# One output projection, two matmul shapes: sixteen 512-column products and a VectorE add in place of sixty-four 128-column products

## The chip, the core and the metric

The kernel runs on one core of a Trainium2 chip. The metric is device time in microseconds (us). A run with a profile also gives a trace; its span (about 656.5 us here) is a little shorter than the device time of the same run (about 658.3 us), since it goes from the first instruction to the last. PE is TensorE, PEld its weight loads, DVE is VectorE, ACT is ScalarE, SPq the queue from which SyncE issues DMA.

## The reference

One decode step: layer norm of a row of 512, then the sum of the row itself, a cached attention block and a dense block.

```python
# x: 1 x 512; wq: 512 x 4096; wo: 4096 x 512
# k_cache, v_cache: 8 groups x 65536 keys x 128; 32 heads, 4 heads in each group
xn = layernorm(x)
q = xn @ wq
o = softmax(q @ K.T / sqrt(128)) @ V          # for each of the 32 heads
out = x + o.reshape(1, 4096) @ wo + gelu(xn @ w1 + b1) @ w2 + b2
```

K and V are 268 MB in bfloat16, wo is 4.2 MB. The step studied here is `o @ wo`, a row of 4096 times a 4096 x 512 matrix, at the very end.

## The kernel before

K and V stream through four SBUF slots while PE transposes K, makes scores and accumulates P times V. The dense branch is finished at the start. Its 512 outputs (with x and b2 in them) wait in `f_rows` as four partial rows, on partitions 0, 32, 64 and 96, with zeros between.

wo is the last thing loaded. It arrives in five pieces: three for the first seven groups (16, 8 and 4 heads: `wo0`, `wo1`, `wo2`) and two for the last group (three heads and one: `wl0`, `wl1`).

```python
def dma_wo():                                       # ... shortened
    for i, (g0, n) in enumerate(WP):                # WP: 4, 2 and 1 groups
        sch.dma(SP, ..., wsem[i], writes=[f"wo{i}"] + (["slot0"] if i == 0 else []))
    for i, n in enumerate(WH):                      # WH: 3 heads and 1
        sch.dma(SP, ..., lsem[i], writes=[f"wl{i}"] + (["slot1"] if i == 0 else []))
```

The tail then multiplies. The stationary operand is one column (one head's share of o), the moving operand a strip of wo. Each of the four 128-column strips of the output goes to its own PSUM partition (0, 32, 64 or 96), called a column group here. Products of the four groups run together in the trace of this kernel: the first four start between 649.637 and 649.657 us, and one takes about 0.31 us. Everything accumulates in one PSUM row per strip, and one VectorE copy and one DMA end the kernel.

```python
def fin_mm(kt, lhsT, rhs, reads, first, last, publish):
    sch.op(PE, lambda: pe.matmul(pR[32 * kt:32 * kt + 1, 0:128], lhsT=lhsT, rhs=rhs, start=first, stop=last), ...)

for kt in range(KT):                                # KT = 4: add the dense branch
    fin_mm(kt, ones_f[:, 0:1], f_rows[:, kt * 128:(kt + 1) * 128], ["f_rows", "ones_f"], True, False, kt == KT - 1)
for i, (g0, n) in enumerate(WP):                    # 64 + 32 + 16 products
    for r in range(g0 * HPG, (g0 + n) * HPG):
        for kt in range(KT):
            fin_mm(kt, oX_bf[:, r:r + 1], wo_sb[:, r, kt * 128:(kt + 1) * 128], ["oX", f"wo{i}"], False, False, ...)
for h in range(HPG):                                # last group: 16 products
    for kt in range(KT):
        fin_mm(kt, oT_all[:, ...], wl_sb[:, h, kt * 128:(kt + 1) * 128], ["oL", "wl0 or wl1"], False, h == HPG - 1, ...)
sch.op(DVE, lambda: dve.tensor_copy(out=fin_bf[0:NR, :], in_=pR[0:NR, 0:128]), ...)   # then the output DMA
```

## Time and profile before

| | before |
|---|---|
| time, median of 3 runs | 658.36 us (658.20 to 658.52) |
| span of the trace | 656.5 us |
| busy: PE, VectorE, ScalarE | 82%, 42%, 37% |
| main DMA queue, share of 16 engines | 99.2% |

PE looks busy, but the DMA engines are the ones that never rest. This is one line of the page's table of DMA queues (queue, packets, MB, share of the 16 engines' span), and the line that sums up HBM traffic:

```profile
q1 hardware_dynamic: 8616, 280.50, 99.2%
...
HBM read 280.50 MB, written 0.00 MB: 427 GB/s over the span
```

The chain of waits (start in us, length, what) ends like this. It is followed backwards from the last instruction, so the first line is what the end was waiting for:

```profile
636.99 16.42 DMA kv<-in_A_wo_dram
653.41 0.14 issue
653.55 0.63 PE pss L805 x13
...
654.20 0.29 DVE fin_bf L820
```

653.41 is the landing of `wl0`. The last piece, `wl1`, lands at 653.73 by the same trace (issued at 637.42, 16.31 us to landing). After these two only the last products, one copy and the output DMA are left. The timeline of the same stretch shows what PE did until then (start, length, engine, line, operation, operands, count, and in brackets the idle time just before with what ended it). A product in fp32 shows as two passes, so the four products with `f_rows` are eight:

```profile
649.26 0.61 PE L805 MATMUL pss<-f_rows,ones_f 128*1 128x128 f32 x8
...
649.64 3.41 PE L805 MATMUL pss<-kv,oX_bf 128*1 128x128 bf16 x112
...
652.45 0.31 PEld L805 LDWEIGHTS pss<-kv,oX_bf 128*1 128x1 bf16 x16 [0.32 <-DMA kv<-in_A_wo_dram]
...
653.55 0.59 PE L805 MATMUL pss<-kv,oT_all 128*1 128x128 bf16 x16 [0.50 <-DMA kv<-in_A_wo_dram]
654.20 0.29 DVE L820 CAST fin_bf<-pss 97x128 bf16<-97x128 f32 x1 [4.13 <-PE pss L805]
```

PE waited twice for wo: 0.32 us for the third piece (seen at the weight loads) and 0.50 us for the last pieces. The granted clock (the share of its full speed that PE is given, 1.00 at most) was 0.50 in all of this, as the table by windows has it (stretch and length in us; busy time and count of PE, PEld, VectorE, ScalarE and GpSimd; then the granted clock of PE, the DMA share and GB/s):

```profile
649.00:651.00 2.00, 2.00 (x73) 1.72 (x73) 0.72 (x5) 0.00 (x0) 0.00 (x0) 0.50 1.02 399
651.00:653.00 2.00, 1.97 (x72) 1.44 (x60) 0.00 (x0) 0.00 (x0) 0.00 (x0) 0.50 0.67 234
```

### The profile page before, as it was taken

How to read it: one execution, taken by the hardware profiler on the slowest of the kernel's cores; microseconds unless marked ns; L12 is line 12 of the kernel's file. 1: busy time of each engine (PE TensorE's matmuls, PEld its weight loads, DVE VectorE, ACT ScalarE, POOL GpSimd, SP SyncE). 2: the span in 40 equal slices, each digit the busy share in tenths (PEclk: the TensorE clock that was granted, in tenths of full speed). 3: DMA queues.
4: the chain of work that ended last, by engine and by line, in shares of the span. 5: the costliest groups of instructions: out<-in, count | busy, mean ns of one | idle time of the engine just before them, and what ended most of it. 6: DMA issues, size and time to landing. Idle time of an engine off the chain costs nothing.

```text
span 656.5 us, 27968 instructions
## 1 busy us (share of the span) xinstructions
PE 539.3 (82%) x12682; PEld 512.1 (78%) x12682; DVE 275.7 (42%) x574; ACT 244.9 (37%) x454; POOL 2.9 (0%) x27
## 2 busy tenths in 40 slices
PE   2388699999789797878969787896978879797897
PEld 0187698988689697868969786896968779686896
DVE  3244162635435172442616245171634516254353
ACT  0134153534425152351605335161443516144251
POOL 0000000000000000000000000000000000000000
PEclk9788597878759596885959778596877859687595
DMA  8999999999999999999999999999999999999997
GB/s 369 438 436 426 429 430 433 439 425 461 401 441 439 421 453 413 437 427 445 433 417 449 417 445 421 427 457 411 447 419 447 429 419 441 423 459 408 431 433 295
DMA packets 8774, 280.65 MB, mean 427 GB/s; under 512 B 1082, under 2 KB 1596, under 8 KB 1724
## 3 DMA queue, kind: packets, MB, share of 16 engines
q1 hardware_dynamic: 8616, 280.50, 99.2%
q8 instruction: 8, 0.13, 0.1%
q10 hardware_dynamic: 148, 0.01, 0.0%
q14 instruction: 2, 0.02, 0.0%
HBM read 280.50 MB, written 0.00 MB: 427 GB/s over the span
## 4 chain that ended last, share of the span: by engine, by line
DMA 63%; PE 34%; issue 2%; DVE 0%; SPq 0%
DMA kv<-in_A_k_cache_dram 61%; PE pst L590 27%; PE pss L610 4%; DMA kv<-in_A_wo_dram 3%; PE pO L681 2%; PE pA L637 0%; PE pA L648 0%; DVE pmax L618 0%; PE pA L697 0%; PE pss L805 0%; DVE gmax L639 0%; DVE diag L641 0%; SPq L470 0%; SPq L467 0%; SPq L463 0%
## 5 line engine op out<-in xcount | busy, mean ns | idle before, releaser
L590 PE MATMUL pst<-ident_bf,kv 128*128 128x128 bf16 x4096 | 284.3, 236 | 34.0 <-DMA kv<-in_A_k_cache_dram 33.9
L600 ACT ACTIVATE kt_ring<-pst 128x1024 bf16<-128x1024 bf16 x192 | 195.6, 1027 | 312.1 <-PE pst L590 310.7
L590 PEld LDWEIGHTS pst<-ident_bf,kv 128*128 128x128 bf16 x4096 | 266.0, 107 | 42.4 <-DMA kv<-in_A_k_cache_dram 35.5
L598 DVE COPY kt_ring<-pst 128x1024 bf16<-128x1024 bf16 x320 | 210.7, 687 | 121.1 <-PE pst L590 118.7
L681 PE MATMUL pO<-P_bf,kv 128*128 128x4 bf16 x4096 | 115.1, 166 | 37.1 <-DMA kv<-in_A_v_cache_dram 32.1
L681 PEld LDWEIGHTS pO<-P_bf,kv 128*128 128x128 bf16 x4096 | 113.6, 104 | 38.5 <-DMA kv<-in_A_v_cache_dram 33.1
L610 PE MATMUL pss<-q_cur,kt_ring 128*128 128x4 bf16 x4096 | 111.9, 164 | 4.9 <-issue 4.9
L610 PEld LDWEIGHTS pss<-q_cur,kt_ring 128*128 128x128 bf16 x4096 | 109.3, 96 | 5.1 <-issue 5.1
L659 ACT ACTIVATE P_bf<-pss,negm 128x128 bf16<-128x128 f32 x128 | 50.9, 547 | 67.6 <-DVE negm L651 67.6
L690 DVE COPY o_all<-pO 128x4 f32 (+1 forms) x32 | 5.2, 161 | 120.3 <-PE pO L681 119.5
L618 DVE TENSOR_REDUCE pmax<-pss 128x4 f32<-128x512 f32 x32 | 22.1, 691 | 68.8 <-PE pss L610 68.8
L659 ACT ACTIVATION_READ_ACCUMULATOR P_bf<-pss,negm 128x1 f32 x128 | 35.3, 276 | 0.0
L648 PEld LDWEIGHTS pA<-diag,ones_f 4*128 4x128 f32 x64 | 12.6, 245 | 17.8 <-DVE diag L641 16.2
L637 PE MATMUL pA<-ident_f,pmax 128*4 128x128 f32 x64 | 14.0, 305 | 12.5 <-DVE pmax L618 12.5
L648 PE MATMUL pA<-diag,ones_f 4*128 4x4 f32 x64 | 15.4, 309 | 10.0 <-DVE diag L641 10.0
L637 PEld LDWEIGHTS pA<-ident_f,pmax 128*4 128x4 f32 x64 | 2.9, 84 | 15.7 <-DVE pmax L618 14.0
L639 DVE TENSOR_REDUCE gmax<-pA 4x1 f32<-4x128 f32 x32 | 8.8, 274 | 9.1 <-PE pA L637 9.1
L673 DVE COPY sums_all<-sums 128x8 f32 (+1 forms) x16 | 2.7, 171 | 23.4 <-ACT P_bf L659 23.4
L697 PE MATMUL pA<-sums_all,ones_f 128*128 128x128 f32 x32 | 12.4, 491 | 0.0
L651 DVE TENSOR_SCALAR negm<-pA 128x4 f32<-128x4 f32 x32 | 5.1, 161 | 10.8 <-PE pA L648 10.8
L697 PEld LDWEIGHTS pA<-sums_all,ones_f 128*128 128x128 f32 x32 | 8.1, 312 | 0.0
L641 DVE TENSOR_SCALAR diag<-ident_f,gmax 4x4 f32<-4x4 f32 x32 | 7.0, 218 | 1.1
(78 smaller groups left out, 49.5 us busy)
## 6 DMA issues: line engine op xcount, KB each, us to landing
kv<-in_A_k_cache_dram SPq DMA_DIRECT2D x32, 4096.0 KB, 27.5
kv<-in_A_v_cache_dram SPq DMA_DIRECT2D x4, 4096.0 KB, 23.2
kv<-in_A_wq_dram SPq DMA_DIRECT2D x1, 4096.0 KB, 12.2
kv<-in_B_w_dram SPq DMA_DIRECT2D x2, 1792.0 KB, 18.0
kv<-in_A_wo_dram SPq DMA_DIRECT2D x1, 2048.0 KB, 23.0
kv<-in_A_wo_dram SPq DMA_DIRECT2D x1, 1024.0 KB, 25.1
kv<-in_A_wo_dram SPq DMA_DIRECT2D x1, 512.0 KB, 25.9
kv<-in_A_wo_dram SPq DMA_DIRECT2D x1, 384.0 KB, 16.4
```

The lines of the kernel that those rows point to most:

```text
L590: lambda tb=tb, at=at, b=b, tt=s * TPB + t: pe.transpose(pst[tb][:, at * 128:(at + 1) * 128], slot[b][:, tt, :], ident_bf[:, :]),
L598: e, fn = DVE, lambda tb=tb, dst=dst: dve.tensor_copy(out=dst, in_=pst[tb][:, :])
L600: e, fn = ACT, lambda tb=tb, dst=dst: act.activation(out=dst, in_=pst[tb][:, :], func=ACTF.Copy)
L610: lambda k=k, kb=kb, at=at, t=t: pe.matmul(pss[k][:, at:at + HPG], lhsT=kt_ring[:, kb * BCOL + t * 128:kb * BCOL + (t + 1) * 128], rhs=q_c ...
L618: lambda k=k: dve.tensor_reduce(out=pmax[:, :], in_=pss[k][:, 0:CW].rearrange("p (t j) -> p j t", j=HPG), axis=AX.X, op=ALU.max),
L637: sch.op(PE, lambda: pe.matmul(pA[0:HPG, PA_ST:PA_ST + 128], lhsT=pmax[:, 0:HPG], rhs=ident_f[:, :], start=True, stop=True), reads=["pmax" ...
L639: sch.op(DVE, lambda: dve.tensor_reduce(out=gmax4[:, :], in_=pA[0:HPG, PA_ST:PA_ST + 128], axis=AX.X, op=ALU.max), reads=["pA"], writes=[" ...
L641: sch.op(DVE, lambda: dve.tensor_scalar(out=diag4[:, :], in0=ident_f[0:HPG, 0:HPG], scalar1=gmax4[0:HPG, 0:1], scalar2=None, op0=ALU.mult) ...
L648: sch.op(PE, lambda: pe.matmul(pA[:, PA_SB:PA_SB + HPG], lhsT=ones_f[0:HPG, 0:128], rhs=diag4[0:HPG, 0:HPG], start=True, stop=True), reads ...
L659: lambda k=k, at=at, j=j, src=src: act.activation(out=P_v[k][:, :, j], in_=src[:, :, j], func=ACTF.Exp, bias=negm[:, at:at + 1], scale=1.0 ...
L681: lambda k=k, t=t: pe.matmul(pO[:, 0:HPG], lhsT=vslot[:, k * TPD + t, :], rhs=P_v[k][:, t, :], start=t == 0, stop=t == TPD - 1),
L697: sch.op(PE, lambda: pe.matmul(pA[:, PA_SUM:PA_SUM + NC], lhsT=ones_f[:, :], rhs=sums_all[:, :], start=True, stop=True), reads=["ones_f", ...
```

## The change

The intent is to do the largest piece of wo with fewer, longer matmuls. For the first sixteen heads, a product covers all 512 columns at once; head r goes to column group r mod 4, so that each of the four PSUM rows holds the sum of four heads. VectorE adds these four rows to the four rows of `f_rows`. The dense branch then enters the final sum later, behind the third piece of wo, through a selector column that is one on partitions 0, 32, 64 and 96. The selector is needed because the other partitions of that PSUM tile hold old scores.

```diff
+    sch.op(DVE, lambda: dve.tensor_reduce(out=row_sel[:, :], in_=ident_f[:, 0:128:32], axis=AX.X, op=ALU.max), ...)
...
-    for kt in range(KT):
-        fin_mm(kt, ones_f[:, 0:1], f_rows[:, kt * 128:(kt + 1) * 128], ["f_rows", "ones_f"], True, False, kt == KT - 1)
+    R0 = WP[0][1] * HPG                              # 16 heads
+    for r in range(R0):
+        c = r % 4
+        sch.op(PE, lambda r=r, c=c: pe.matmul(pss[1][32 * c:32 * c + 1, :], lhsT=oX_bf[:, r:r + 1], rhs=wo_sb[:, r, :],
+                                              start=r < 4, stop=r >= R0 - 4), ...)
+    sch.op(DVX, lambda: dve.tensor_tensor(out=f_rows[:, :], in0=pss[1][:, :], in1=f_rows[:, :], op=ALU.add), ...)
     for i, (g0, n) in enumerate(WP):
+        if i == 0:
+            continue
         ...                                          # 32 + 16 products as before
+    for kt in range(KT):
+        fin_mm(kt, row_sel[:, :], f_rows[:, kt * 128:(kt + 1) * 128], ["f_rows", "row_sel"], False, False, kt == KT - 1)
```

More of the change, by code (lines that the diff above doesn't have):

```diff
@@ L368, in bass_parallel_sum__gqa_block_cached__dense_activation_gelu__decode_kernel @@
     part_r = [sb(f"part_r{i}", [128, n * HPG], BF) for i, (_, n) in enumerate(WP)]
+    row_sel = sb("row_sel", [128, 1], F32)
     flag = sb("flag", [1, 1], F32)
@@ L783, in bass_parallel_sum__gqa_block_cached__dense_activation_gelu__decode_kernel @@
                 reads=["ident_f"], writes=[res])
+    sch.op(DVE, lambda: dve.tensor_reduce(out=row_sel[:, :], in_=ident_f[:, 0:128:32], axis=AX.X, op=ALU.max),
+           reads=["ident_f"], writes=["row_sel"])
     marks, marks2 = [], []
@@ L806, in fin_mm @@
                reads=reads, writes=[f"pss{R}"], publish=publish)
-    for kt in range(KT):
-        fin_mm(kt, ones_f[:, 0:1], f_rows[:, kt * 128:(kt + 1) * 128], ["f_rows", "ones_f"], True, False, kt == KT - 1)
+    R0 = WP[0][1] * HPG
+    for r in range(R0):
+        c = r % 4
+        sch.op(PE, lambda r=r, c=c: pe.matmul(pss[1][32 * c:32 * c + 1, :], lhsT=oX_bf[:, r:r + 1], rhs=wo_sb[:, r, :],
+                                              start=r < 4, stop=r >= R0 - 4),
+               reads=["oX", "wo0"], writes=["pss1"], publish=r == R0 - 1)
+    sch.op(DVX, lambda: dve.tensor_tensor(out=f_rows[:, :], in0=pss[1][:, :], in1=f_rows[:, :], op=ALU.add),
+           reads=["pss1", "f_rows"], writes=["f_rows"])
     for i, (g0, n) in enumerate(WP):
+        if i == 0:
+            continue
         for r in range(g0 * HPG, (g0 + n) * HPG):
             for kt in range(KT):
-                fin_mm(kt, oX_bf[:, r:r + 1], wo_sb[:, r, kt * 128:(kt + 1) * 128], ["oX", f"wo{i}"], False, False,
+                fin_mm(kt, oX_bf[:, r:r + 1], wo_sb[:, r, kt * 128:(kt + 1) * 128], ["oX", f"wo{i}"], r == R0, False,
                        r == (g0 + n) * HPG - 1 and kt == KT - 1)
+    for kt in range(KT):
+        fin_mm(kt, row_sel[:, :], f_rows[:, kt * 128:(kt + 1) * 128], ["f_rows", "row_sel"], False, False, kt == KT - 1)
     for h in range(HPG):
```

## The prediction

> **What bounds the kernel now.** The DMA stream. The table of DMA queues gives the main queue 99.2% of the 16 engines' span, 280.5 MB at 427 GB/s. The chain of waits is 63% DMA and ends "DMA kv<-wo 16.42 us, landing at 653.41; issue 0.14; PE 0.63; DVE 0.29"; the output is issued at 654.52. After the last piece of wo lands, only sixteen matmuls, one eviction and the output DMA remain.
>
> **The tail before, from the timeline (PE at granted clock 0.50).**
> - 649.26: f_rows x ones, 8 fp32 passes, two groups of four 0.16 us apart, hidden in the wait for the oX cast (ends 649.57).
> - 649.64: 64 + 32 products for the first two wo pieces, 107 ns per round of four column groups, until about 652.2.
> - The weight load waits 0.32 us for the third piece (lands about 652.4); its 16 products run from 652.45 to 653.05.
> - PE waits 0.50 us for the next piece; the last 16 products run from 653.55 to 654.14.
>
> **What the change removes, adds, moves.**
> - 64 products of 128 columns become 16 of 512. At the kernel's start, 32 products of 512 columns in the same four-group form start 107 ns apart (3.53 us for all). Sixteen then take 16 x 0.107 = 1.71 us; the 64 take 16 rounds x 0.107 = 1.71 us. No PE time is saved: the four groups stream the same number of columns. [...]
> - Added: a VectorE add of 128x512 from PSUM, about 0.69 us (the f_rows copy, same shape and source, took 0.69), from about 651.6 to 652.35, while PE does the second piece.
> - Moved: the 8 fp32 f_rows passes, from a free place (649.26) to after the third piece: from about 652.88, for 0.35 to 0.45 us, done by about 653.3. That fits in the 0.50 us wait, with about 0.2 us over.
> - Added: one tiny VectorE reduction (below 0.4 us) at about 27 us, where VectorE idles until 33.6 us.
>
> **On the critical path.** None of the saving, and none of the cost unless the fp32 passes overrun the last landing: at worst 0.2 us. DMA order, sizes and triggers (slot reads by the transposes) are unchanged.
>
> **Predicted time.** 658.4 us, range 657.5 to 659.4 (mostly run to run; the spread before is 0.3 us). Faster by over 2%: 0.5%; within 2%: 98.5%; slower: 1%.
>
> **What would show each step right or wrong.**
> - DMA: the same 280.5 MB at about 427 GB/s, last wo landing about 1 us after the third piece's and about 3.1 us before the span's end.
> - PE: the 16 wide products span about 2 us, 427 ns per round of four.
> - The f_rows passes stand after the third piece, waiting for nothing or for wo, not for VectorE; the chain still ends DMA wo, last products, eviction, output.
> - The last products' wait for the DMA shrinks from 0.50 to 0.1 to 0.3 us.
>
> **What would make it wrong.**
> - A full clock in the tail: PE ends earlier but waits for the same landing; the time holds.
> - The fp32 passes waiting for the VectorE add, or taking over 0.6 us: up to 0.5 us slower.
> - A DMA rate differing by run or chip by over 0.15% moves the time by over 1 us, outside the change.

Either form was put at 16 x 107 ns = 1.71 us, from the spacing that the trace of the kernel before shows for narrow products in the tail and for wide ones at the kernel's start, so the saving comes to 0; the VectorE add (0.69 us) and the fp32 passes (0.35 to 0.45 us) were put inside waits, so the change adds 0, and 658.4 us is the time before. Two figures have their measurement only after the change: the 427 ns per round of four (four times 107 ns; rounds start at 649.49 and 649.91 in the trace after) and the reduction below 0.4 us (0.15 us, at 27.57).

## The result, and the profile after

| | before | after |
|---|---|---|
| time, median (range), 4 runs each | 658.37 us (658.20 to 658.52) | 658.30 us (658.06 to 659.51) |
| span of the profiled run | 656.5 us | 656.4 us |
| PE busy | 539.3 us | 536.7 us |
| instructions | 27,968 | 27,873 |
| mean granted clock | 0.767 | 0.769 |

The ratio of the changed kernel's time to the time before is 1.0003, with a 95% interval of 0.9985 to 1.0020. A ratio here is the mean time of one kernel's fast runs over that of the other's fast runs of the same rounds, so it is not quite the ratio of the medians. (The run of 659.51 us has a core span of 656.4 us: its extra microsecond lies outside the span.)

The queue table has the same 280.50 MB, at 427 GB/s. The timeline of the tail after the change, with the same columns as before:

```profile
649.10 1.87 PE L814 MATMUL pss<-kv,oX_bf 128*1 128x512 bf16 x16 [0.30 <-DVE oX_bf L801]
...
651.03 0.69 DVE L817 TENSOR_TENSOR f_rows<-pss,f_rows 128x512 f32<-128x512 f32 x1 [1.49 <-PE pss L814]
...
651.19 1.02 PE L808 MATMUL pss<-kv,oX_bf 128*1 128x128 bf16 x32 [0.21 <-DMA kv<-in_A_wo_dram]
...
652.48 0.59 PE L808 MATMUL pss<-kv,oX_bf 128*1 128x128 bf16 x16 [0.26 <-DMA kv<-in_A_wo_dram]
...
652.86 0.64 PE L808 MATMUL pss<-f_rows,row_sel 128*1 128x128 f32 x8
653.46 0.41 PEld L808 LDWEIGHTS pss<-kv,oT_all 128*1 128x1 bf16 x16 [0.47 <-DMA kv<-in_A_wo_dram]
653.46 0.55 PE L808 MATMUL pss<-kv,oT_all 128*1 128x128 bf16 x16
654.06 0.29 DVE L833 CAST fin_bf<-pss 97x128 bf16<-97x128 f32 x1 [2.33 <-PE pss L808]
```

In this run PE reached the tail half a microsecond sooner (649.10 against 649.64) and simply waited for the second piece as well. The weight loads of the last products still start when the DMA lets them, at 653.46, against 653.52 before. The eight fp32 passes stand in what had been the 0.50 us wait. While the wide products ran, the granted clock was 0.50, as it was before:

```profile
649.00:651.00 2.00, 1.87 (x16) 0.37 (x16) 0.48 (x4) 0.00 (x0) 0.00 (x0) 0.50 1.00 393
```

The chain of waits shows how thin the margin is; it now leaves the DMA earlier, at the third piece:

```profile
625.96 26.48 DMA kv<-in_A_wo_dram
652.43 0.04 issue
652.48 1.56 PE pss L808 x25
...
654.06 0.29 DVE fin_bf L833
```

From the third piece's landing to the end PE has no gap as modelled, so the chain never meets the last two landings. The weight loads still do: those of the last head start at 653.78, right behind the landing of the very last piece (issued at 636.90, 16.84 us to landing, so at 653.74). In the kernel before, that landing was at 653.73 and these loads started at 653.77. PE and DMA now end this tail almost together; the runs without the wo loads, below, show how much room is left.

### The profile page after: what moved, and what is told of

Same layout as the page of the kernel before. It is cut to its first block, busy times and chain, and to the rows that moved or that the text cites. A ratio compares the mean times of both kernels' runs of the same rounds, so it can differ in the third digit from the quotient of the medians.

```text
span 656.4 us, 27873 instructions
## 1 busy us (share of the span) xinstructions
PE 536.7 (82%) x12634; PEld 507.4 (77%) x12634; DVE 276.3 (42%) x576; ACT 245.0 (37%) x454; POOL 2.9 (0%) x27
## 3 DMA queue, kind: packets, MB, share of 16 engines
q1 hardware_dynamic: 8616, 280.50, 99.3%
HBM read 280.50 MB, written 0.00 MB: 427 GB/s over the span
## 4 chain that ended last, share of the span: by engine, by line
DMA 69%; PE 29%; issue 2%; SPq 0%; DVE 0%
DMA kv<-in_A_k_cache_dram 65%; PE pst L591 24%; DMA kv<-in_A_wo_dram 4%; PE pss L611 3%; PE pO L682 1%; PE pss L808 0%; PE pA L638 0%; PE pA L649 0%; SPq L479 0%; DVE pmax L619 0%; PE pA L698 0%; SPq L471 0%; SPq L468 0%; SPq L464 0%; DVE gmax L640 0%
## 5 line engine op out<-in xcount | busy, mean ns | idle before, releaser
L591 PE MATMUL pst<-ident_bf,kv 128*128 128x128 bf16 x4096 | 280.8, 234 | 34.8 <-DMA kv<-in_A_k_cache_dram 34.7
L591 PEld LDWEIGHTS pst<-ident_bf,kv 128*128 128x128 bf16 x4096 | 262.5, 106 | 43.2 <-DMA kv<-in_A_k_cache_dram 36.4
L649 PEld LDWEIGHTS pA<-diag,ones_f 4*128 4x128 f32 x64 | 12.6, 245 | 18.2 <-DVE diag L642 16.5
```

Source lines behind the costliest of these rows:

```text
L591: lambda tb=tb, at=at, b=b, tt=s * TPB + t: pe.transpose(pst[tb][:, at * 128:(at + 1) * 128], slot[b][:, tt, :], ident_bf[:, :]),
L649: sch.op(PE, lambda: pe.matmul(pA[:, PA_SB:PA_SB + HPG], lhsT=ones_f[0:HPG, 0:128], rhs=diag4[0:HPG, 0:HPG], start=True, stop=True), reads ...
```

## The experiments

Theory T: the landing of the last wo pieces fixes the end. Four column groups stream the same number of columns either way, so PE saves nothing, and the change only reorders work inside a wait. Rival R1: the wide products do save PE time, and the VectorE add and the late fp32 passes give it back. Rival R2: there is a small effect that the few runs hid. Further theories came up on the way and are named where they did.

### The changed kernel again, five rounds (after_again)

No edit.

> The changed kernel again, five rounds against the kernel before on one chip. Theory T (the landing of the last wo pieces fixes the end; the change only reorders work inside a wait): ratio 0.9995 to 1.0005. Rival R1 (the wide products do save PE time in the tail, but the VectorE add and the late fp32 passes give it back): the same total, so this run does not tell them apart; it sets the noise for the others. Rival R2 (the change saves or costs a few tenths of a us at the end): ratio outside 0.9995 to 1.0005 by more than the interval.

Measured: 658.38 us (658.35 to 658.54) against 658.34 us, ratio 1.0000, interval 0.9986 to 1.0014. R2 is bounded by 0.14% either way, about 0.9 us. The trace agrees more closely than the times can: the last products start at 653.74 (653.55 before), right behind a DMA landing (the fourth piece, issued at 637.22, 16.5 us to landing).

### Only the fp32 passes moved (move_alone)

```diff
-    for kt in range(KT):
-        fin_mm(kt, ones_f[:, 0:1], f_rows[...], ["f_rows", "ones_f"], True, False, kt == KT - 1)
     ...                              # 64 + 32 + 16 narrow products; the first of each strip now has start=True
+    for kt in range(KT):
+        fin_mm(kt, ones_f[:, 0:1], f_rows[...], ["f_rows", "ones_f"], False, False, kt == KT - 1)
```

> The kernel before, with only the eight fp32 f_rows passes moved to after the third wo piece; narrow products kept, no VectorE add. T: within 0.2 us of before (658.2 to 658.6), and the trace shows the last products' idle time before them shrink from 0.50 us to about 0. R1: the late passes cost what the wide products save, so this one alone is slower by 0.4 us or more, about 658.8.

Measured: 658.39 us (658.23 to 658.44), ratio 1.0000 (0.9986 to 1.0014). By itself the move costs nothing that can be seen, against R1. The timeline of this run:

```profile
648.80 1.87 PE L805 MATMUL pss<-kv,oX_bf 128*1 128x128 bf16 x64 [0.50 <-DMA kv<-in_A_wo_dram]
...
652.69 0.39 PE L805 MATMUL pss<-f_rows,ones_f 128*1 128x128 f32 x8
...
653.57 0.46 PE L805 MATMUL pss<-kv,oT_all 128*1 128x128 bf16 x16 [0.49 <-DMA kv<-in_A_wo_dram]
```

The first line isolates the 64 narrow products, because here PE had to wait for the second piece behind them: 1.87 us at a granted clock of 0.50, by the table by windows of this run:

```profile
649.00:651.00 2.00, 1.67 (x64) 1.38 (x52) 0.04 (x1) 0.00 (x0) 0.00 (x0) 0.50 0.99 389
```

The sixteen wide ones of the changed kernel took 1.87 us at the same clock. That is the prediction's central claim, read off two lines.

One part of the expectation failed. The wait of the last products did not shrink to about 0; it stayed at 0.49 us. In this run the clock rose to full at about 652.1 (0.72 on average from 651 to 653 us), so the passes were done sooner. A faster PE waited longer for the same landing, and the end did not move.

### Fewer column groups (groups_2, groups_1)

```diff
-        c = r % 4
+        c = r % 2                    # or r % 1
-                                              start=r < 4, stop=r >= R0 - 4),
+                                              start=r < 2, stop=r >= R0 - 2),
...                                   # the add takes only the partitions that were written
```

> The changed kernel with the sixteen wide products in two column groups instead of four. T: what counts is columns streamed per group, so they take about 16 x 427 / 2 = 3.4 us instead of 1.7; from a start at 649.1 to 649.6 all PE work then ends about 0.8 to 1.3 us later than before (slack used up), 659.2 to 659.7, and the last products no longer wait for the DMA. If the cost went by the number of products, or if PE time in the tail did not matter at all: unchanged, 658.3.

> The same with all sixteen in one column group. T: at least 16 x 427 = 6.8 us for the products, the end about 4.2 to 4.8 us later than in the changed kernel, 662.5 to 663.2 (more if weight loads into the same group no longer overlap). By number of products, or with PE off the path entirely: unchanged.

Both take 427 ns from one wide product of a column group to its next. In the trace of groups_2 the weight loads of successive rounds stand at 650.03, 650.46, 650.89, 651.31 and 651.74, so 427 ns apart at a granted clock of 0.50. Weight loads overlapped in one group too: in groups_1 PE was busy for 2.00 of the 2.00 us from 651 to 653 us, and PEld for 0.63 of them.

Measured with two groups: 658.59 us (658.04 to 660.12), ratio 1.0003 (0.9990 to 1.0017). The expected 0.8 to 1.3 us did not show in the median. The profiled run, the slowest of the five, has the eviction at 655.11 and a span of 657.5 us, 1.0 us longer than before; the other four have spans of 656.2 to 657.1 us. So this dose sits at the edge of the slack, and the timing is inconclusive.

Measured with one group: 660.50 us (659.58 to 662.11), ratio 1.0037 (1.0023 to 1.0051). Slower, so PE is not off the path entirely and the number of instructions is not what counts. But the increase is 2.2 us where 4.2 to 4.8 was expected. The timeline and the clock explain a good part of the difference:

```profile
648.91 5.40 PE L814 MATMUL pss<-kv,oX_bf 128*1 128x512 bf16 x14 [0.30 <-DVE oX_bf L801]
...
654.14 0.38 PE L814 MATMUL pss<-kv,oX_bf 128*1 128x512 bf16 x1
...
654.36 0.38 PE L814 MATMUL pss<-kv,oX_bf 128*1 128x512 bf16 x1
```

The table by windows of the same run:

```profile
651.00:653.00 2.00, 2.00 (x6) 0.63 (x5) 0.00 (x0) 0.00 (x0) 0.00 (x0) 0.50 0.63 222
653.00:655.00 2.00, 2.00 (x48) 0.98 (x47) 0.22 (x1) 0.00 (x0) 0.00 (x0) 0.89 0.01 3
```

While the clock was 0.50 the wide products of one group started 427 ns apart (the weight loads of this stretch stand at 649.29, 649.72, 650.14 and so on). At about 653.45 the clock went to full; the last two started 0.22 us apart, and all that followed ran at full clock too (1.00 from 655 to 657 us). My expectation had carried the half clock to the end: at 427 ns apiece the last wide product would have started at 655.3 instead of 654.36.

### Without the wo loads (before_no_wo, after_no_wo)

Both kernels with the five wo loads left out. The products read old K data, so the result is wrong. Nothing in the tail waits for a DMA then, and PE and VectorE alone set the end.

```diff
             if kind == "W":
-                dma_wo()
                 return
```

> The kernel before without its five wo loads (stale K in their place, a wrong result on purpose), so that nothing in the tail waits for a DMA and VectorE's and PE's own time sets the end. T: from a start of the products near 649.6 (or 0.5 us earlier) 128 products at 27 ns and a last latency of 0.31 us end at about 653.4 instead of 654.1: 0.5 to 1.0 us faster than before, about 657.6. If the tail were bound by the DMA alone with PE far from it: many us faster.

> The changed kernel without its wo loads. T: at the half clock the wide products take as long as the narrow ones, and the eight fp32 passes now stand in the line (about 0.4 us), so from the first product to the eviction it takes about 0.4 us longer than before_no_wo, about 658.0. R1 (the wide form saves PE time, hidden so far by the wait for the DMA): shorter than before_no_wo by 0.4 us or more.

Measured: before without wo 657.00 us (656.86 to 657.40), ratio 0.9979 (0.9965 to 0.9993); changed without wo 657.20 us (656.12 to 657.92), ratio 0.9976 (0.9962 to 0.9990). The times do not tell the two apart. (Both medians lie below what was expected, 657.6 and 658.0, by 0.6 and 0.8 us; why was not examined.) The timelines, of one profiled run each, do. Before without wo:

```profile
649.22 3.21 PE L804 MATMUL pss<-kv,oX_bf 128*1 128x128 bf16 x112
...
652.21 0.65 PE L804 MATMUL pss<-kv,oT_all 128*1 128x128 bf16 x16
652.90 0.29 DVE L819 CAST fin_bf<-pss 97x128 bf16<-97x128 f32 x1 [3.25 <-PE pss L804]
```

Changed without wo:

```profile
649.45 1.87 PE L813 MATMUL pss<-kv,oX_bf 128*1 128x512 bf16 x16 [0.30 <-DVE oX_bf L800]
651.11 1.49 PE L807 MATMUL pss<-kv,oX_bf 128*1 128x128 bf16 x48
...
652.39 0.64 PE L807 MATMUL pss<-f_rows,row_sel 128*1 128x128 f32 x8
652.82 0.64 PE L807 MATMUL pss<-kv,oT_all 128*1 128x128 bf16 x16
653.51 0.29 DVE L832 CAST fin_bf<-pss 97x128 bf16<-97x128 f32 x1 [1.44 <-PE pss L807]
```

From the first product to the eviction it is 3.68 us before and 4.06 us changed, both at a granted clock of 0.50 throughout. The changed tail is 0.38 us longer on PE, as T had it (about 0.4): the wide products save nothing and the fp32 passes now stand in the line. R1 wanted it shorter by 0.4 us or more, and falls. The pair also shows how close PE follows the DMA: with 4.2 MB less to load, 9.8 us of DMA at 427 GB/s, the kernels gain only 1.1 to 1.3 us.

It also gives the room that the fp32 passes leave in the changed kernel. Without wo the last products start 0.43 us after the passes (652.39 to 652.82), with no landing to wait for. In the changed kernel itself it was 0.60 us (652.86 to 653.46, and the same in after_again), so there the landing still held them back by about 0.17 us.

### The first piece nine times, narrow and wide (narrow_x9, wide_x9)

To measure the disputed cost by itself, the first piece is multiplied nine times in each form; the result stays right.

```diff
# narrow, in the kernel before: eight extra passes into the other PSUM tile, not used
+    for rep in range(8):
+        for r in range(16):
+            for kt in range(KT):
+                sch.op(PE, ... pe.matmul(pss[1][32 * kt:32 * kt + 1, 0:128], lhsT=oX_bf[:, r:r + 1],
+                                         rhs=wo_sb[:, r, kt * 128:(kt + 1) * 128], start=r == 0, stop=r == 15) ...)
# wide, in the changed kernel
+    for rep in range(9):
         for r in range(R0):
             ...
```

> The kernel before, with the 64 narrow products of the first piece done nine times (eight into the other PSUM tile, not used). T with the clock as seen in the last runs (half for some 4 us after the products start, then full, where narrow products started 20 ns apart instead of 27): about 2.5 repeats at 1.71 us and 6.5 at 1.28 us, 12.6 us in all, the end about 9.5 us later than before, 667 to 668.5.

> The changed kernel with the sixteen wide products done nine times. T: the same as narrow ones at half clock (1.71 us a repeat), but 0.86 us a repeat at full clock (214 ns per round of one column group in the last run), 9.9 us in all; the end about 6.9 us later than before, 664.5 to 666, some 2 to 3 us faster than narrow_x9. If wide and narrow cost the same at any clock: equal to narrow_x9. If the wide form were already cheaper at half clock: faster than narrow_x9 by over 4 us.

The run that both call the last is groups_1. There the products started at 648.91 and the clock went to full at about 653.45, 4.5 us later; after that the last two wide products started 0.22 us apart, for which the expectation has 214 ns, and 42 narrow ones took 1.04 us, so (1.04 - 0.22) / 41 = 20 ns from start to start.

Measured: narrow 669.93 us (669.74 to 670.47), ratio 1.0178; wide 664.58 us (663.89 to 665.47, four runs), ratio 1.0098. The wide form is now 5.35 us faster. By the letter of the expectation this should mean that it was already cheaper at half clock, which the 1.87 us readings contradict. The wide time fell inside its range (664.5 to 666); the narrow one was 1.4 us above the top of its own (668.5). The chain of waits of the narrow run shows something else:

```profile
649.12 5.02 PE pss L811 x218
654.14 0.09 issue
654.23 1.96 PE pss L811 x128
656.18 1.78 issue
657.97 1.96 PE pss L811 x128
659.93 1.51 issue
661.44 0.72 PE pss L811 x38
662.16 1.34 PE pss L805 x90
663.50 1.40 issue
```

There are three gaps, 4.69 us in all, in which PE waits for nothing that the profile shows. Each comes after 128 products. In between, products start (1.96 - 0.22) / 127 = 13.7 ns apart (one product lasts 0.22 us). In the trace of the wide run, at full clock, a column group took its next product every 216 ns (24 rounds of four from 652.78 to 657.96), so 54 ns for one with four groups at work, and a quarter of that is 13.5 ns. So at full clock too a narrow product costs about a quarter of a wide one while it flows. The table of DMA queues for 648 to 667 us of this run has the instruction queue in use:

```profile
q8 instruction: 5, 0.08, 1.7%
```

Five transfers of 16 KB. Three of them begin at 655.30, 659.00 and 662.53, about 0.9 us before each gap opens, and last 1.0 to 1.2 us. A product is two instructions (weight load and matmul), so 128 products are 256 instructions (the timeline counts 128 of each in the stretches from 654.23 and from 657.97). The stretch from 661.44 to the last gap, 38 and 90 products in the chain, makes 128 too, so each gap comes after 256 instructions. New theory I: the gaps are instruction supply, not the array. Rival A: the array takes narrow products more slowly.

### The narrow repeats in a loop (narrow_loop)

```diff
-    ...                              # eight straight copies of the 64 narrow products
+    ...                              # one straight copy, then
+    with pe.Fori(0, 7):
+        for r in range(16):
+            for kt in range(KT):
+                narrow(r, kt)
```

> narrow_x9 with the extra eight repeats of the 64 narrow products as one straight copy and a loop of seven[...]. In the trace of narrow_x9 PE stood idle for 1.78, 1.51 and 1.40 us with nothing to wait for, each time after 128 products (256 instructions), while at full clock its products started 13.7 ns apart. Theory I (those gaps are the supply of instructions, and narrow and wide products cost the same per column at either clock): no such gaps in the repeats, and the time within about 1.5 us of wide_x9's 664.6, 664 to 666. Theory A (the array itself takes narrow products more slowly at full clock): unchanged, 669 to 670.

Measured: 664.55 us (664.26 to 665.49, four runs), ratio 1.0099 (1.0083 to 1.0114). It fell by 5.4 us and landed on the wide form's 664.58 us. The chain of waits has no gap left. First the loop, then the wide run (wide_x9):

```profile
648.71 9.54 PE pss L809 x509
658.25 2.03 PE pss L805 x136
```

```profile
648.85 9.53 PE pss L815 x135
...
658.40 0.70 DVE f_rows L818
```

Theory I holds, A falls. The same products, executed equally often, cost 5.4 us less from a loop, and the instruction queue shows two transfers from 648 to 662 us (0.03 MB) in place of five from 648 to 667 us (0.08 MB). Why a gap comes after just 256 instructions was not shown. Within a turn of the loop they started 13.3 ns apart at full clock, a quarter of the 54 ns of a wide one. (The loop also drops the semaphore update after each repeat of 64 products. The gaps came every 128 products, so this is not a likely cause, but it was not tested by itself.)

The agreement to 0.03 us is partly luck. The eight narrow repeats of the first line take as long as nine wide ones, in part because the loop loses time between turns (0.16 to 0.20 us from product to product at full clock). Against that, the wide kernel has the exposed VectorE add, 0.7 us in its chain.

### The VectorE add made late (add_late)

```diff
+    for rep in range(4):
+        sch.op(DVX, lambda: dve.tensor_copy(out=h_rows[...], in_=pss[1][...]), reads=["pss1"], writes=["h_rows"])
     sch.op(DVX, lambda: dve.tensor_tensor(out=f_rows[:, :], in0=pss[1][:, :], in1=f_rows[:, :], op=ALU.add), ...)
```

> The changed kernel with four extra VectorE copies of the same PSUM tile (0.69 us each) ahead of the add. T says that the add had about 1.0 us to spare in the changed kernel (it ended at 651.72, the fp32 passes started at 652.75 to 652.86), so 2.76 us more put it about 1.7 us past that: the fp32 passes then wait for VectorE at about 654.6 and the end comes 1.1 to 1.7 us later, 659.4 to 660. If VectorE did not matter for the end: 658.3.

Measured: 659.62 us (658.99 to 660.18), ratio 1.0021 (1.0007 to 1.0035), 1.4 us later, in the expected range. The timeline shows the wait that the changed kernel does not have:

```profile
653.42 0.68 DVE L820 TENSOR_TENSOR f_rows<-pss,f_rows 128x512 f32<-128x512 f32 x1
654.16 0.10 PEld L808 LDWEIGHTS pss<-f_rows,row_sel 128*1 128x1 f32 x8 [1.47 <-DVE f_rows L820]
```

So the add is hidden in the changed kernel because it has time to spare (1.0 us in the first profiled run, where it ended at 651.72 and the weight loads of the passes started at 652.75; 0.6 us in after_again), not because VectorE could never matter.

## Why the prediction was right

- **DMA fixes the end.** Right. The bytes, the rate and the last two landings (653.41 and 653.73 before, 653.42 and 653.74 after) are unchanged, and in the run with the passes moved alone a full clock from 652.1 on did not bring the end forward. It needs one qualification that the prediction did not make: without wo the kernels gain only 1.1 to 1.3 us, since PE follows close behind.
- **No PE time saved.** Right: 1.87 us for 16 wide products, 1.87 us for 64 narrow ones, both at granted clock 0.50. Products of different column groups ran together: in the changed kernel four wide products started within 0.01 us of one another in each round (rounds at 649.49 and 649.91). With one group in place of four the wide products started 427 ns apart, one in the time of four.
- **"If the clock were full, PE would end earlier but wait for the same landing."** Right: moved alone, at full clock, the last products waited 0.49 us.
- **VectorE add hidden.** Right in length (0.69 us), half a microsecond earlier than predicted (651.03 to 651.72), because this run's PE reached the tail earlier.
- **The moved fp32 passes fit in the wait.** Right, and so was the margin, although the timeline hides it. It shows the passes as 0.64 us long (652.86 to 653.50) and no idle time before the last matmuls, but the end of the passes can overlap the next products: in the run without wo the passes are 0.64 us long too (652.39 to 653.03), and the next products started at 652.82. What the passes take of PE is the 0.43 us after which the last products started in the run without wo; forecast were 0.35 to 0.45 us. The wait that is left is the 0.17 us by which the landing held the last products back beyond that (a difference between two runs); forecast were 0.1 to 0.3 us.
- **The wait for the second piece** (0.21 us) was not predicted. It is again PE that came early and stood still.

What stays open: any effect below about 0.1% in the time. The trace puts the last products' start within 0.3 us (653.46 to 653.74) in the four profiled runs of the two kernels and of the moved passes, each right behind a landing.

## What to carry to other kernels

Count the columns streamed through each column group, not the matmuls: here sixteen products of 512 columns in four groups took 1.87 us, as did sixty-four of 128 columns, both at granted clock 0.50. Longer products pay in another currency, instructions: in narrow_x9 PE stood idle for 1.4 to 1.8 us after every 256 instructions of straight-line code at full clock, and there, with the products done nine times, the wide form, or a loop, was worth 5 us. Before shortening a tail, ask what its last products wait for. Here it was a DMA landing, and time saved ahead of it turned into idle time ahead of it (0.49 us in move_alone).

## What else the traces show

- Instructions, in narrow_x9: PE stood idle for 1.4 to 1.8 us after each 256 instructions of straight-line code and resumed 3.5 to 3.7 us apart, so that a weight load and its matmul took 27 to 29 ns with the gaps counted in, against 13.7 ns from start to start between the gaps (128 products in 1.96 us). The loop of 64 products had no such gap.
- The clock, in the kernel before: it was 1.00 from 630 to 636 us, where PE was transposing most of the time (5.3 of 6.00 us). PE was busy for 0.72 of the 2.00 us from 639 to 641 us, with 0.78 us as the longest idle time. The mean clock was 0.61 from 641.0 to 641.5 us and 0.50 from there to the end, although PE was busy by the profile for 3.87 of the 4.00 us from 641 to 645 us, mostly with 4-column products (3.5 us). So busy time as the profile counts it did not keep the clock up here; what does was not shown.
